# Ten V units of a cached attention in five transfers of 8 MB, with K in two slots of its own

## The chip, the cores and the metric

The kernel runs on one core of one Trainium2 chip. The metric is the device time of one execution in microseconds (us). A profile of one execution lies beside the times; line numbers such as L694 are lines of the kernel before.

## The reference

Two blocks read the same eight rows `x` (8 x 576) and are mixed by a gate. Block A is attention with one query per sequence over the last 2048 keys of a cache; block B is a layer norm, a 576 to 4608 projection, a GELU and the projection back.

```python
g = sigmoid((x * gate_w).sum(-1))
q = (x @ wq).reshape(8, 1, 32, 128)                 # 32 query heads, 16 K/V heads
k = repeat(k_cache[:, :, 8192 - 2048:, :], 2)       # 8 x 16 heads x 2048 keys x 128
v = repeat(v_cache[:, :, 8192 - 2048:, :], 2)
p = softmax(q @ k.T * 128 ** -0.5)
a = (p @ v).reshape(8, 4096) @ wo
h = gelu(layernorm(x) @ w1 + b1)
b = h @ w2 + b2
out = g * a + (1 - g) * b
```

All is bf16 in memory. The window of K and of V is 67 MB each; the weights are about 20 MB.

## The kernel before

**Units.** K and V are each read in 16 units of 4 MB. Unit n belongs to group g = n // 4 (32 of the 128 pairs of sequence and K/V head) and holds 512 of the 2048 keys of these pairs. In SBUF a unit is 128 partitions x 32 KB: four partitions per pair, 128 keys in each. The kernel walks through four groups of four units and rescales a running sum `O` from unit to unit; at the end of a group the accumulated result is reduced and written into a matrix that the output projection reads.

**Slots.** `RAW` has `ND = 4` slots of 32 KB per partition. `take_slot` deals them out in the turn 1, 2, 0, 3, to K and V alike. `load_item` (L623 to L630) issues one transfer on SP's queue, which waits for `slot_free[s]`: for a K unit its four transposes, for a V unit its PV matmuls. The order of transfers is `stream` (L590 to L594 and L603): K0 K1 V0 K2 V1 K3 V2 ... K15 V14 V15, then the weights of the last projections. The first weights lie in slots 0 and 3 and are read before.

**A K unit** (`k_unit`). Four times (a "quarter" below, `tr` and `qk` in the code): VectorE transposes 128 x 2048 words (L694) into one of two buffers in `KT`, and PE adds eight matmuls (L712 and L175) to four banks of scores, in which a mask lies already. The transpose of a quarter waits for the matmuls of the second quarter before it, whose buffer it takes.

**Softmax** (`softmax`, `spread`). VectorE takes the maximum (L645) and the bias (L647, L649), ScalarE makes the exponentials P (L651), and then writes the mask into the banks for the next unit (L655). VectorE transposes P into one of two halves of `PT` (L669). At the end of a group a short chain of small steps forms the sums (L675 to L682).

**A V unit** (`v_item`). POOL and ScalarE copy P into a matrix with zeros between ("spread P", L743 and L744: `qrx`), whose one home lies at the end of `RAW`; unit 15 uses `KT`, which is cleared for that (L727). Then PE runs 64 matmuls (`pv`: L757, and L186 in a loop with registers), and VectorE adds the result to `O` (L798, L800: `o`). After the last unit of a group it forms the group's result (L803, L806, L808: `vmul`, `acc`, `ew`) and PE adds it to a bank (L811: `us`).

**What sets the order.** Each engine's instructions stand in a fixed order, written by the planner `_Plan.schedule`: it takes the operations by estimated start, from the costs that are given with each, and from a model of the transfers (`DMA_BW`, `DMA_LAT`). At run time every operation waits for its `deps` by semaphores, in that order; `after` only acts on the planner.

**The end.** Behind V15 come b2, 3.4 MB of w2, wo in two transfers and the rest of w2 (L833, L850, L862). Their matmuls (L583) all add to one bank, which is written out at L892 to L897.

Of the kernel before, what the change touches and what calls it, by code (L numbers as in the profile page):

```python
# [6 lines left out]
BF = mybir.dt.bfloat16  # L7
# [30 lines left out]

class _Plan:

    DMA_BW = 428e3
    DMA_LAT = 1.8
    DMA_ISSUE = 0.35
    SEM_LAT = 0.08

# [16 lines left out]
    def schedule(self):  # L62
        n = len(self.all)
        done = [False] * n
        eng_free = {e: 0.0 for e in ENGS}
        dma_free = 0.0
        remaining = set(range(n))
        npred = [0] * n
        succ = [[] for _ in range(n)]
        for op in self.all:  # L70
            preds = set(d.idx for d in op.deps) | set(d.idx for d in op.after)
            npred[op.idx] = len(preds)
            for p in preds:
                succ[p].append(op.idx)
        ready = [i for i in range(n) if npred[i] == 0]
        count = 0
        while ready:
            best = None
            best_key = None
            for i in ready:  # L80
                op = self.all[i]
                r = 0.0
                for d in op.deps:
                    r = max(r, d.t1 + self.SEM_LAT)
                for d in op.after:
                    r = max(r, d.t0)
                est = max(eng_free[op.eng], r)
                key = (est - 0.2 * op.prio, -op.prio, i)
                if best_key is None or key < best_key:
                    best_key = key  # L90
                    best = i
            op = self.all[best]
            ready.remove(best)
            est = max([eng_free[op.eng]] + [d.t1 + self.SEM_LAT for d in op.deps] + [d.t0 for d in op.after])
            op.t0 = est
            if op.is_dma:
                eng_free[op.eng] = est + op.cost
                if op.nbytes < 65536:
                    op.t1 = est + 0.4 + self.DMA_LAT
                else:  # L100
                    start = max(est + 0.4, dma_free)
                    dma_free = start + op.nbytes / self.DMA_BW
                    op.t1 = dma_free + self.DMA_LAT
            else:
                op.t1 = est + op.cost
                eng_free[op.eng] = op.t1
            op.pos = len(self.order[op.eng])
            self.order[op.eng].append(op)
            done[best] = True
            count += 1  # L110
            for s_ in succ[best]:
# [12 lines left out]
        for e in ENGS:  # L124
            for op in self.order[e]:
                if op.is_dma:
                    cnts[op.dma_sem] = cnts.get(op.dma_sem, 0) + 1
                    op.dma_val = 16 * cnts[op.dma_sem]
        needed = set()
        for op in self.all:  # L130
            for d in op.deps:
                if not d.is_dma:
                    needed.add(d.idx)
        for e in ENGS:
            c = 0
# [57 lines left out]
def build_kernel(nc, A_x, A_k_cache, A_v_cache, A_wq, A_wo, B_x, B_w1, B_b1, B_w2, B_b2, gate_w, out):  # L193
# [22 lines left out]
    WO_CH = 16  # L216
    JN = D // NJ
    BIG = 1.0e9
    x2 = A_x.rearrange("b s d -> (b s) d")
    out2 = out.rearrange("b s d -> (b s) d")  # L220

    with ExitStack() as es:
# [15 lines left out]
        req("ones_bf", 512, BF)  # L238
        req("zeros_bf", 128, BF)
        req("maskL", 128, BF)  # L240
        req("maskR", 512, BF)
# [8 lines left out]
        req("pair", 128, F32)  # L250
        req("selv", 136, F32)
        req("maskhd", 4, F32)
        req("r8", 128, F32)
        req("idf8", 8, F32)
        req("dg", 16, F32)
        req("sel", 4 * 128, BF)
        req("sel4", 128, BF)
        req("cols", 16, F32)
        req("xT", 6 * 32, BF)
        req("yT", 6 * 32, BF)  # L260
        req("q4", 4 * 256, BF)
        req("qbd", 4 * 4 * 128, BF)
        req("b2", D, BF)
        req("uh", FCW, F32)
        req("v1", FCW, F32)
        req("hT", FT * 32, BF)
        req("ob", 16, BF)
        req("ot32", 8, F32)
# [1 line left out]
        req("sm", 8 * NL, F32)  # L270
        req("sg", 8 * NG, F32)
        req("gcol", 1, F32)
        req("on", 512, BF)
        req("O", 256, F32)
        req("EW", 512, F32)
        req("EV", 128, F32)
        req("oT", 512, BF)
        req("out_sb", JN, BF)
# [4 lines left out]
        over("vm", "uh", 0, 256, F32)  # L283
        over("x_sb", "PT", 0, D, BF)
        over("gw_sb", "PT", 1152, D, BF)
        over("y_bf", "PT", 2304, D, BF)
# [64 lines left out]
        EV, Oc = view("EV"), view("O")  # L351
        RAW = view("RAW")
        PX = aoffs("RAW") + ND * DE
        ptx_f = bass.AP(arena_f, offset=PX // 2, ap=[[AST // 2, 128], [1, 4096]])
        x_sb, gw_sb, y_bf = view("x_sb", 8), view("gw_sb", 8), view("y_bf", 8)
        xz = view("xz", 8).rearrange("p (s c) -> p s c", s=2)
        yz = view("yz", 8).rearrange("p (s c) -> p s c", s=2)
# [3 lines left out]
        def slot(s):  # L361
            return RAW[:, s * DE:(s + 1) * DE]
# [248 lines left out]
        pt_done, px_done, pv_done = {}, {-1: [o_px0]}, {}  # L611
# [4 lines left out]
        px_engs = [("pool", "pool", "act", "act")] * (NL - 2) + [("act", "dve", "dve", "dve"), ("act", "dve", "dve", "dve")]  # L616

        def take_slot():
            n = n_slot[0]
            n_slot[0] += 1  # L620
            return (1, 2, 0, 3)[n % ND]

        def load_item(cache, nm, n):  # L623
            s = take_slot()
            g, i = divmod(n, 4)
            src = cache.rearrange("b h s d -> (b h) s d")[32 * g:32 * g + 32, S0 + KL * i:S0 + KL * i + KL, :].rearrange("j (x r) d -> j x (r d)", x=4)
            d = dma("sp", lambda e: e.dma_start(slot(s), src), "s%d" % s, 8 * W * Dh * 2, deps=slot_free[s], name="%s%d" % (nm, n), after=last_dma[-1:])
            last_dma.append(d)
            slot_free[s] = []
            return s, d  # L630

        def query(g):
            qb_done[g] = []
# [52 lines left out]
        def k_unit(n, s, d):  # L686
            g, i = divmod(n, 4)
            trs = []
            for rh in range(2):
                for hh in range(2):  # L690
# [33 lines left out]
            if n == NL - 1:  # L724
                o_kz.deps.append(qk)

        o_kz = add("pool", lambda e: e.memset(view("KT").bitcast(F32), 0.0), deps=[], name="ktx0", cost=4.5, prio=3)  # L727

        def v_item(n):
            s, d = load_item(A_v_cache, "dv", n)  # L730
            g, i = divmod(n, 4)
            if n == NL - 1:
                spread(n)
            ob_ = BK_OS[n % 2]
            px_at = aoffs("KT") if n == NL - 1 else PX
            px_free = [o_kz] if n == NL - 1 else [pv_done.get(n - 1), o_px0]
            px_done[n] = []
            for c in range(4):
                def fn(e, c=c):
# [6 lines left out]

            if n == NL - 2:
                mx_done[n + 1].after.extend(op for op in px_done[n] if op.eng == "dve")
                o_kz.deps.extend(op for op in px_done[n] if op.eng == "dve")

            def pv_part(a, b):
                def fn(e):
# [30 lines left out]
            if n >= NL - 2:  # L783
                after.append(keep_warm("warm_pv%d" % n, (10, 6)[n - NL], after, (ob_,), [o_u, o_done[n - 2]]))
            if n < NL - 1:
                pv = add("pe", lambda e: pv_looped(e, 64, 2, 6 if n < NL - 2 else 12), deps=deps, name="pv%d" % n, cost=8.2, after=after)
            else:
                pva = add("pe", lambda e: pv_looped(e, 48, 4, 14), deps=deps, name="pv%da" % n, cost=5.4, after=after)
# [4 lines left out]
            slot_free[s] = [pv]  # L793
# [89 lines left out]
        pv_hist = []  # L883
        query(0)
        for kind, i in stream:
            {"K": k_item, "V": v_item, "W": wo_all, "M": m2_chunk, "B": bias}[kind](i)

        acc_ops = [g_.op for g_ in acc_groups]
        fin = []
# [61 lines left out]
```

## Time and profile before

| | before |
|---|---|
| median of 3 runs | 364.59 us (364.51 to 364.76) |
| the profiled execution | 364.57 us |
| its span | 363.3 us |
| mean granted TensorE clock | 0.92 |
| busy: PE, DVE, ACT, POOL | 78%, 71%, 36%, 20% of the span |
| moved by the DMA engines | 154.45 MB, mean 425 GB/s |
| K and V transfers | 16 + 16 of 4096 KB, 26.4 and 26.3 us from issue to landing (median) |
| chain that ended last, by engine | DMA 50%, DVE 35%, PE 9%, issue 4%, ACT 2% |

The span runs from the first to the last instruction; the execution's own time is 1.27 us longer. The time from issue to landing holds the wait in the queue behind earlier transfers. The clock is that which the chip granted to TensorE, 1.00 or 0.50 in any moment.

### The profile page before, as it was taken

Reading aid. Unit: us, or ns where it says so; the run is one execution under the profiler, and the core shown is the slowest. Engines: PE = TensorE matmul, PEld = TensorE weight load, DVE = VectorE, ACT = ScalarE, POOL = GpSimd, SP = SyncE. Lnnn points to the kernel's source line nnn. Section 1 sums busy time; section 2 is a strip of 40 time slices with the busy share of each in tenths; the row PEclk is TensorE's granted clock in tenths of the full one; section 3 lists DMA queues with packets and bytes.
Section 4 is the critical chain, followed back from the end, with each engine's and each line's share of the span. In section 5 each row is a group of like instructions: output and inputs, shape, how many; then the busy total and the mean of one; then the engine's idle time right before and its main releaser. Section 6 shows DMA issues by size and latency. Waiting matters only on the chain.

```text
span 363.3 us, 4428 instructions
## 1 busy us (share of the span) xinstructions
PE 284.4 (78%) x1842; PEld 126.6 (35%) x1381; DVE 257.3 (71%) x201; ACT 131.8 (36%) x117; POOL 73.5 (20%) x72
## 2 busy tenths in 40 slices
PE   0355554999897967997978949897969679978996
PEld 0110000436171703452432607170706034513763
DVE  0722978797978596959495878677695979498530
ACT  1012106274544440735342434444444416313300
POOL 9123002230414040302212030404040403003000
PEclk9976596999998997999896998998999899999999
DMA  8999999999999999999999999999999999999995
GB/s 349 433 440 402 462 404 459 404 462 404 462 404 460 404 462 408 456 411 451 413 451 415 451 415 451 415 451 413 447 419 451 415 451 412 449 415 447 412 440 234
DMA packets 6146, 154.45 MB, mean 425 GB/s; under 512 B 716, under 2 KB 884, under 8 KB 1272
## 3 DMA queue, kind: packets, MB, share of 16 engines
q1 hardware_dynamic: 6080, 154.29, 98.7%
q8 instruction: 6, 0.10, 0.1%
q10 hardware_dynamic: 56, 0.03, 0.0%
q14 instruction: 4, 0.03, 0.0%
HBM read 154.31 MB, written 0.01 MB: 425 GB/s over the span
## 4 chain that ended last, share of the span: by engine, by line
DMA 50%; DVE 35%; PE 9%; issue 4%; ACT 2%; ACTq 0%; POOL 0%; SPq 0%
DMA arena<-in_A_k_cache_dram 42%; DVE arena L694 20%; DMA arena<-in_B_w_dram 5%; DVE arena L669 5%; PE ps L175 4%; DMA arena<-in_gate_w_dram 2%; DVE arena L645 2%; PE ps L186 2%; DVE arena L803 1%; PE ps L505 1%; PE ps L712 1%; DVE arena L800 1%; DVE arena L566 1%; DVE arena L808 1%; ACT arena L651 1%
## 5 line engine op out<-in xcount | busy, mean ns | idle before, releaser
L694 DVE STREAM_TRANSPOSE arena<-arena 128x2048 f32<-128x2048 f32 x64 | 145.0, 2288 | 23.6 <-DMA arena<-in_A_k_cache_dram 20.9
L175 PE MATMUL ps<-arena 128*128 128x512 bf16 (+2 forms) x461 | 131.2, 436 | 0.0
L186 PE MATMUL ps<-arena 128*128 x942 | 106.1, 274 | 0.1
L712 PE MATMUL ps<-arena 128*128 128x512 bf16 x128 | 54.6, 426 | 54.4 <-DVE arena L694 47.7
L186 PEld LDWEIGHTS ps<-arena 128*128 x942 | 92.4, 98 | 11.6 <-issue 0.6
L744 POOL COPY arena<-arena 32x2048 bf16<-32x2048 bf16 x28 | 52.8, 1884 | 211.1 <-DVE arena L669 210.3
L743 ACT ACTIVATE arena<-arena 32x2048 bf16<-32x2048 bf16 x30 | 57.2, 1906 | 64.3 <-DVE arena L669 64.0
L651 ACT ACTIVATE arena<-ps,arena 128x2048 bf16<-128x2048 f32 x16 | 31.5, 1967 | 113.1 <-DVE arena L649 78.5
L712 PEld LDWEIGHTS ps<-arena 128*128 128x128 bf16 x128 | 13.5, 105 | 159.0 <-DVE arena L694 98.1
L645 DVE TENSOR_REDUCE arena<-ps 128x1 f32<-128x2048 f32 x16 | 36.7, 2292 | 35.4 <-PE ps L175 35.4
L669 DVE STREAM_TRANSPOSE arena<-arena 128x2048 bf16<-128x2048 bf16 x16 | 36.4, 2274 | 2.1 <-ACT arena L651 2.1
L655 ACT ACTIVATE ps<-arena 128x2048 f32<-128x2048 f32 x15 | 28.1, 1873 | 0.1
L757 PE MATMUL ps<-arena 128*128 128x256 bf16 x82 | 14.5, 276 | 1.0 <-DVE arena L744 1.0
L757 PEld LDWEIGHTS ps<-arena 128*128 128x128 bf16 x82 | 8.0, 100 | 19.0 <-issue 17.1
L455 PE MATMUL ps<-arena 8*128 8x8 bf16 x8 | 0.6, 171 | 14.6 <-DVE arena L429 9.5
L583 PE MATMUL ps<-arena 128*8 128x288 bf16 (+1 forms) x140 | 9.6, 286 | 1.6 <-DMA arena<-in_A_wo_dram 0.6
L561 DVE TENSOR_TENSOR arena<-arena 128x1152 f32<-128x1152 f32 x1 | 1.4, 1358 | 11.5 <-ACT arena L559 11.5
L727 POOL MEMSET arena<- 128x4096 f32 x1 | 3.5, 3510 | 22.7 <-DVE arena L744 22.7
L583 PEld LDWEIGHTS ps<-arena 128*8 128x8 bf16 (+1 forms) x140 | 5.7, 86 | 5.9 <-DMA arena<-in_B_w_dram 1.3
L638 POOL COPY arena<-arena 32x128 bf16<-32x128 bf16 x16 | 4.6, 287 | 15.0 <-ACT arena L540 7.4
L429 DVE COPY arena<-arena 8x64 bf16<-8x64 bf16 x2 | 0.3, 190 | 9.1 <-DMA arena<-in_gate_w_dram 9.1
L800 DVE SCALAR_TENSOR_TENSOR arena<-arena,ps 128x256 f32<-128x256 f32 x12 | 5.3, 446 | 1.4 <-PE ps L757 1.4
(106 smaller groups left out, 98.9 us busy)
## 6 DMA issues: line engine op xcount, KB each, us to landing
arena<-in_A_k_cache_dram SPq DMA_DIRECT2D x16, 4096.0 KB, 26.4
arena<-in_A_v_cache_dram SPq DMA_DIRECT2D x16, 4096.0 KB, 26.3
arena<-in_B_w_dram SPq DMA_DIRECT2D x1, 4608.0 KB, 23.3
arena<-in_A_wo_dram SPq DMA_DIRECT2D x2, 2304.0 KB, 20.6
arena<-in_A_wq_dram SPq DMA_DIRECT2D x1, 4096.0 KB, 12.9
arena<-in_B_w_dram SPq DMA_DIRECT2D x1, 3456.0 KB, 26.6
arena<-in_B_w_dram SPq DMA_DIRECT2D x1, 1152.0 KB, 19.6
arena<-in_B_w_dram SPq DMA_DIRECT2D x1, 576.0 KB, 24.2
```

The source lines that it names most:

```text
L175: return e.add_instruction(mybir.InstMatmult(name=nc.get_next_instruction_name(), engine=mybir.EngineType.PE, ins=[e.lower_ap(rhs), e.lowe ...
L186: return e.add_instruction(mybir.InstMatmult(name=nc.get_next_instruction_name(), engine=mybir.EngineType.PE, ins=[operand(r, r_ap), opera ...
L583: ins = e.matmul(ps[32 * j:32 * j + 8, BK_ACC, 0:JN], lhsT, rhs[:, JN * j:JN * j + JN], start=False, stop=True, skip_group_check=True, til ...
L645: mx = mx_done[n] = add("dve", lambda e: e.tensor_reduce(out=k(n, MX), in_=ps[:, 0:4, :].rearrange("p a n -> p (a n)"), axis=AXL.X, op=ALU ...
L651: ex = add("act", lambda e: e.activation(out=Pm, in_=ps[:, 0:4, :].rearrange("p a n -> p (a n)"), func=ACTF.Exp, bias=k(n, NB), scale=SCAL ...
L655: mask_done[n + 1] = add("act", lambda e: e.activation(out=ps[:, 0:4, :].rearrange("p a (n c) -> p (a n) c", c=32), in_=bass.AP(arena_f, o ...
L669: pt_done[n] = add("dve", lambda e: e.transpose(bass.AP(arena, offset=aoffs("PT") + 2048 * (n % 2), ap=[[AST, 128], [1, 2048]]), Pm), deps ...
L694: tr = add("dve", (lambda rh=rh, hh=hh, kb=kb: lambda e: e.transpose(bass.AP(arena_f, offset=foffs("KT") + kb * 2048, ap=[[AST // 2, 128], ...
L712: mm = e.matmul(*args, start=False, stop=True, skip_group_check=True) if rc == 0 else held_matmul(nc, e, *args, stop=True, skip=True)
L743: return e.activation(out=dst, in_=src, func=ACTF.Copy)
L744: return e.tensor_copy(dst, src)
L757: mm = e.matmul(ps[:, ob_, 0:256], lhsT, rhs, start=(k == 0), stop=True, skip_group_check=True)
```

## The change

Ten of the sixteen V units, 2 to 11, come in five transfers of two units each (`P2`, `P4`, `P6`, `P8`, `P10`): 128 partitions x 64 KB into slots 2 and 3 together. Such a transfer waits for the PV matmuls of both units that lay there. The partition of the keys follows: a partition holds 256 consecutive keys of a pair, 128 of each of two neighbouring units, so a transfer of one unit now reads every second run of 32 KB. K units use slots 1 and 0 in turn, V units 2 and 3; the turn through four slots is gone. The order of transfers is written out in `STREAM`.

Spread P has two homes, by the parity of the unit, one at the end of `RAW` and one in `PXB`; both are cleared at the start, and the copies of unit n wait for PV n-2 instead of n-1. The clearing of `KT` for unit 15 is gone. To make room, several small tiles share memory. The planner's model of transfers and the costs of `qk` and `pv` have other numbers, and the loop body of two PVs near the end is 6 matmuls long instead of 12 and 14.

```diff
-    DMA_BW = 428e3
-    DMA_LAT = 1.8
+    DMA_BW = 433.2e3
+    DMA_LAT = 0.45
+    DMA_START = 1.7
...
-                    start = max(est + 0.4, dma_free)
+                    start = max(est + self.DMA_START, dma_free)
...
+    STREAM = "K0 K1 V0 K2 V1 K3 K4 P2 K5 K6 P4 K7 K8 P6 K9 K10 P8 K11 K12 P10 K13 K14 V12 V13 K15 V14 V15"
...
+        req("PXB", SE, BF)
...
-        ptx_f = bass.AP(arena_f, offset=PX // 2, ap=[[AST // 2, 128], [1, 4096]])
+        PXS = (PX, aoffs("PXB"))
...
-        stream = [("K", 0), ("K", 1)]
-        for vi in range(NL):
-            stream.append(("V", vi))
-            if vi + 2 < NL:
-                stream.append(("K", vi + 2))
+        stream = [(k[0], int(k[1:])) for k in STREAM.split()]
...
-        o_px0 = add("pool", lambda e: e.memset(ptx_f, 0.0), deps=[o_qp, o_hp], name="ptx0", cost=4.5)
-        n_slot = [0]
+        px_zero = [add("pool", (lambda k=k: lambda e: e.memset(bass.AP(arena_f, offset=PXS[k] // 2, ap=[[AST // 2, 128], [1, 4096]]), 0.0))(), deps=[o_qp, o_hp] + [o_hf] * k, name="ptx%d" % k, cost=4.5) for k in range(2)]
+        late_slots = [1, 0, 2]
...
-        def load_item(cache, nm, n):
-            s = take_slot()
+        def load_item(cache, nm, n, s, both=False):
             g, i = divmod(n, 4)
-            src = cache.rearrange("b h s d -> (b h) s d")[32 * g:32 * g + 32, S0 + KL * i:S0 + KL * i + KL, :].rearrange("j (x r) d -> j x (r d)", x=4)
-            d = dma("sp", lambda e: e.dma_start(slot(s), src), "s%d" % s, 8 * W * Dh * 2, deps=slot_free[s], name="%s%d" % (nm, n), after=last_dma[-1:])
+            keys = cache.rearrange("b h s d -> (b h) s d")[32 * g:32 * g + 32, S0 + 2 * KL * (i // 2):S0 + 2 * KL * (i // 2) + 2 * KL, :]
+            if both:
+                src, dst = keys.rearrange("j (x r) d -> j x (r d)", x=4), RAW[:, s * DE:(s + 2) * DE]
+            else:
+                src, dst = keys.rearrange("j (x u r) d -> u j x (r d)", x=4, u=2)[n % 2], slot(s)
+            free = slot_free[s] + (slot_free[s + 1] if both else [])
+            d = dma("sp", lambda e: e.dma_start(dst, src), "s%d" % s, (1 + both) * 8 * W * Dh * 2, deps=free, name="%s%d" % (nm, n), after=last_dma[-1:])
...
-                    qk = add("pe", qk_fn, deps=deps, name="qk%d_%d%d" % (n, rh, hh), cost=1.85, after=qk_half[-1:] + pv_hist[-1:])
+                    qk = add("pe", qk_fn, deps=deps, name="qk%d_%d%d" % (n, rh, hh), cost=1.75, after=qk_half[-1:] + pv_hist[-1:])
...
         def v_item(n):
-            s, d = load_item(A_v_cache, "dv", n)
+            v_unit(n, 2 + n % 2, load_item(A_v_cache, "dv", n, 2 + n % 2))
+
+        def v_pair(n):
+            d = load_item(A_v_cache, "dv", n, 2, both=True)
+            for u in range(2):
+                v_unit(n + u, 2 + u, d)
+
+        def v_unit(n, s, d):
...
-            px_at = aoffs("KT") if n == NL - 1 else PX
-            px_free = [o_kz] if n == NL - 1 else [pv_done.get(n - 1), o_px0]
+            px_at = PXS[n % 2]
+            px_free = [pv_done.get(n - 2), px_zero[n % 2]]
...
-                pv = add("pe", lambda e: pv_looped(e, 64, 2, 6 if n < NL - 2 else 12), deps=deps, name="pv%d" % n, cost=8.2, after=after)
+                pv = add("pe", lambda e: pv_looped(e, 64, 2, 6), deps=deps, name="pv%d" % n, cost=7.1, after=after)
...
         def k_item(n):
-            s, d = load_item(A_k_cache, "dk", n)
-            k_unit(n, s, d)
+            s = 1 - n % 2
+            k_unit(n, s, load_item(A_k_cache, "dk", n, s))
```

More of the change, by code (lines that the diff above doesn't have):

```diff
@@ L98, in schedule @@
                 if op.nbytes < 65536:
-                    op.t1 = est + 0.4 + self.DMA_LAT
+                    op.t1 = est + 0.4 + 1.8
                 else:
-                    start = max(est + 0.4, dma_free)
+                    start = max(est + self.DMA_START, dma_free)
                     dma_free = start + op.nbytes / self.DMA_BW
@@ L237, in build_kernel @@
         req("ident", 128, BF)
-        req("ones_bf", 512, BF)
+        req("EW", 512, F32)
+        over("ones_bf", "EW", 0, 512, BF)
+        over("sel", "EW", 1024, 4 * 128, BF)
         req("zeros_bf", 128, BF)
@@ L252, in build_kernel @@
         req("maskhd", 4, F32)
-        req("r8", 128, F32)
         req("idf8", 8, F32)
         req("dg", 16, F32)
-        req("sel", 4 * 128, BF)
         req("sel4", 128, BF)
         req("cols", 16, F32)
-        req("xT", 6 * 32, BF)
-        req("yT", 6 * 32, BF)
+        req("early", 640, BF)
+        over("xT", "early", 0, 6 * 32, BF)
+        over("yT", "early", 384, 6 * 32, BF)
+        over("r8", "early", 768, 128, F32)
+        over("b2", "early", 0, D, BF)
         req("q4", 4 * 256, BF)
         req("qbd", 4 * 4 * 128, BF)
-        req("b2", D, BF)
-        req("uh", FCW, F32)
-        req("v1", FCW, F32)
+        req("vm", 256, F32)
+        req("PXB", SE, BF)
+        over("uh", "PXB", 0, FCW, F32)
+        over("v1", "PXB", 4 * FCW, FCW, F32)
         req("hT", FT * 32, BF)
@@ L272, in build_kernel @@
         req("gcol", 1, F32)
-        req("on", 512, BF)
         req("O", 256, F32)
-        req("EW", 512, F32)
         req("EV", 128, F32)
-        req("oT", 512, BF)
-        req("out_sb", JN, BF)
         req("PT", 2 * 2048, BF)
@@ L282, in build_kernel @@
         req("RAW", ND * DE + SE, BF, 512)
-        over("vm", "uh", 0, 256, F32)
+        over("on", "P", 0, 512, BF)
+        over("oT", "P", 1024, 512, BF)
+        over("out_sb", "PT", 0, JN, BF)
         over("x_sb", "PT", 0, D, BF)
@@ L606, in build_kernel @@
         slot_free = [[o_qp], [], [], [o_hp]]
-        o_px0 = add("pool", lambda e: e.memset(ptx_f, 0.0), deps=[o_qp, o_hp], name="ptx0", cost=4.5)
-        n_slot = [0]
+        px_zero = [add("pool", (lambda k=k: lambda e: e.memset(bass.AP(arena_f, offset=PXS[k] // 2, ap=[[AST // 2, 128], [1, 4096]]), 0.0))(), deps=[o_qp, o_hp] + [o_hf] * k, name="ptx%d" % k, cost=4.5) for k in range(2)]
+        late_slots = [1, 0, 2]
         tr_hist, qk_half = [], []
         qk_unit, qb_done = {}, {}
-        pt_done, px_done, pv_done = {}, {-1: [o_px0]}, {}
+        pt_done, px_done, pv_done = {}, {}, {}
         ex_done, nb_done, al_done, ss_done, o_done = {}, {}, {}, {}, {}
@@ L618, in take_slot @@
         def take_slot():
-            n = n_slot[0]
-            n_slot[0] += 1
-            return (1, 2, 0, 3)[n % ND]
-        def load_item(cache, nm, n):
-            s = take_slot()
-            g, i = divmod(n, 4)
-            src = cache.rearrange("b h s d -> (b h) s d")[32 * g:32 * g + 32, S0 + KL * i:S0 + KL * i + KL, :].rearrange("j (x r) d -> j x (r d)", x=4)
-            d = dma("sp", lambda e: e.dma_start(slot(s), src), "s%d" % s, 8 * W * Dh * 2, deps=slot_free[s], name="%s%d" % (nm, n), after=last_dma[-1:])
+            return late_slots.pop(0)
+        def load_item(cache, nm, n, s, both=False):
+            g, i = divmod(n, 4)
+            keys = cache.rearrange("b h s d -> (b h) s d")[32 * g:32 * g + 32, S0 + 2 * KL * (i // 2):S0 + 2 * KL * (i // 2) + 2 * KL, :]
[5 more added lines that the diff above has]
+            d = dma("sp", lambda e: e.dma_start(dst, src), "s%d" % s, (1 + both) * 8 * W * Dh * 2, deps=free, name="%s%d" % (nm, n), after=last_dma[-1:])
             last_dma.append(d)
             slot_free[s] = []
-            return s, d
+            if both:
+                slot_free[s + 1] = []
+            return d
         def query(g):
@@ L723, in k_unit @@
             softmax(n)
-            if n == NL - 1:
-                o_kz.deps.append(qk)
-        o_kz = add("pool", lambda e: e.memset(view("KT").bitcast(F32), 0.0), deps=[], name="ktx0", cost=4.5, prio=3)
         def v_item(n):
-            s, d = load_item(A_v_cache, "dv", n)
+            v_unit(n, 2 + n % 2, load_item(A_v_cache, "dv", n, 2 + n % 2))
[4 more added lines that the diff above has]
+        def v_unit(n, s, d):
             g, i = divmod(n, 4)
@@ L748, in v_item @@
                 mx_done[n + 1].after.extend(op for op in px_done[n] if op.eng == "dve")
-                o_kz.deps.extend(op for op in px_done[n] if op.eng == "dve")
             def pv_part(a, b):
@@ L785, in v_item @@
             if n < NL - 1:
-                pv = add("pe", lambda e: pv_looped(e, 64, 2, 6 if n < NL - 2 else 12), deps=deps, name="pv%d" % n, cost=8.2, after=after)
+                pv = add("pe", lambda e: pv_looped(e, 64, 2, 6), deps=deps, name="pv%d" % n, cost=7.1, after=after)
             else:
-                pva = add("pe", lambda e: pv_looped(e, 48, 4, 14), deps=deps, name="pv%da" % n, cost=5.4, after=after)
+                pva = add("pe", lambda e: pv_looped(e, 48, 4, 6), deps=deps, name="pv%da" % n, cost=5.4, after=after)
                 sums[g].after.append(pva)
@@ L792, in v_item @@
             pv_done[n] = pv
-            slot_free[s] = [pv]
+            slot_free[s] = slot_free[s] + [pv]
             al = sm[:, n, 3:4]
@@ L885, in build_kernel @@
         for kind, i in stream:
-            {"K": k_item, "V": v_item, "W": wo_all, "M": m2_chunk, "B": bias}[kind](i)
+            {"K": k_item, "V": v_item, "P": v_pair, "W": wo_all, "M": m2_chunk, "B": bias}[kind](i)
         acc_ops = [g_.op for g_ in acc_groups]
```

## The prediction, made before the changed kernel ran

> **What bounds it now.** I read first the slices of the span and the waits of the queue that issues the transfers, then the chain of waits, the order of time around one group's end, and the granted clock by windows. The profiled execution took 364.57 us, its span 363.3; the runs' median is 364.59, so sums against the one hold for the other.
>
> ```profile
> DMA  8999999999999999999999999999999999999995
> ...
> SPq L627 <- DVE arena L694: 114.8, 12, 17.3
> SPq L627 <- PE ps L757: 94.3, 10, 11.4
> ```
>
> The DMA engines are full to the end. SP waits for buffers all the time (us in total, times, longest) and it costs nothing: a 4 MB transfer lands 26.4 us after its issue (page, DMA issues) though it moves for only 9.7. The queue is some 16 us ahead, and that cover hides every late matmul.
>
> ```profile
> 204.10 2.27 DVE arena L694
> 206.37 2.19 DVE arena L669
> 208.57 2.19 DVE arena L694
> 210.76 0.38 DVE arena L800
> 211.16 1.59 DVE arena L803
> 212.77 0.43 DVE arena L806
> 213.23 0.69 DVE arena L808
> 213.92 2.23 DVE arena L694
> ```
>
> In the chain of waits (start, duration) VectorE runs without a gap: K transposes (L694), P's (L669), and at a group's end 2.7 us of accumulation (L803 to L808) ahead of the unit's fourth transpose.
>
> ```profile
> 138.85 0.61 PE L712 MATMUL ps<-arena 128*128 128x512 bf16 x1 [2.99 <-DVE arena L694]
> ...
> 140.53 0.63 PE L712 MATMUL ps<-arena 128*128 128x512 bf16 x1
> ...
> 142.18 2.29 DVE L645 TENSOR_REDUCE arena<-ps 128x1 f32<-128x2048 f32 x1 [3.39 <-PE ps L175]
> 142.84 0.38 PE L757 MATMUL ps<-arena 128*128 128x256 bf16 x2
> ...
> 144.70 1.97 ACT L651 ACTIVATE arena<-ps,arena 128x2048 bf16<-128x2048 f32 x1 [9.61 <-DVE arena L649]
> ...
> 146.84 1.87 ACT L655 ACTIVATE ps<-arena 128x2048 f32<-128x2048 f32 x1
> ...
> 149.82 0.39 PE L712 MATMUL ps<-arena 128*128 128x512 bf16 x1
> ...
> 150.72 0.39 PE L712 MATMUL ps<-arena 128*128 128x512 bf16 x1
> ```
>
> These rows of the timeline are my prices. Four QK matmuls take 0.90 us (149.82 to 150.72), a quarter of a unit (eight) 1.8; the same four took 1.68 at 138.85. A PV takes 7.0 (142.84 to 149.82), exp up to the next mask 2.1 (144.70 to 146.84), the mask 1.9, the maximum 2.3, a transpose 2.2. The handoff from PE to VectorE or SP costs about 0.2, others 0.05 to 0.1.
>
> ```profile
> 131.40:134.90 3.50, 1.43 (x7) 0.19 (x2) 3.46 (x3) 3.48 (x2) 3.44 (x2) 0.99 0.98 421
> 134.90:138.30 3.40, 0.95 (x3) 0.00 (x0) 3.33 (x4) 0.19 (x1) 0.21 (x1) 0.50 0.83 357
> 138.30:141.70 3.40, 2.85 (x7) 0.25 (x2) 0.49 (x1) 0.00 (x0) 0.00 (x0) 0.50 1.05 453
> ```
>
> In the windows (length, PE busy, PEld, DVE, ACT, POOL, clock, DMA) a window of 3.4 us with PE busy for 1.43 is followed by half clock, and a well filled one ends it. Today that also hides behind the queue.
>
> **What the change saves.** In the trace's packets a row of 32 KB takes 1213 ns and one of 36 KB 1364: 151 ns for 4 KB more, so some 5 ns of a row are fixed. Five merged transfers have 8 fewer rows per DMA engine each: 40 x 5 to 9 ns = 0.2 to 0.35 us; I take 0.25. Transfers already follow each other every 9.69 us, 8 x 1.21, so five fewer issues save nothing more. If the chip cuts the rows at 32 KB, the 0.25 is gone.
>
> **What it costs.** A pair overwrites both V slots, so its issue waits for both PVs of the pair before. Those can start only when that pair has landed, with only two K transfers (19.4 us) queued behind it; today each slot has its own wait and 16 us of lead. The transfers behind the issue on SP's queue wait too. K's own slots are free in time: K4, the tightest, waits for K2's transposes, done at 83.1 (today's K4 issue waits for the same at 83.12), and the queue runs dry at about 85. P2 waits for the second PV, done at 92.1 today, against 94.8: no hole. The start of a transfer on an empty queue isn't in the steady part of this trace; the first one, 0.5 MB, landed 3.5 us after issue, of which 1.2 is data, so issue to first byte is between 0 and 2.3. The first packets begin 1.0 after the issue and all engines are at work by 1.25; I take 1.15.
>
> The second home of spread P removes a wait of the copies (L743, L744) for the PV before. In today's timeline they start 0.1 after the transpose L669, so this is worth nothing by itself. It is what lets PV n+1 follow PV n at once; without it 4 us more would stand between them. Moving constants and memsets lies in the first 35 us or on POOL, 20% busy: nothing.
>
> **The loop from one pair to the next.** In the changed program PE's order is: PV 3, K5's four quarters, K6's first three, PV 4, K6's fourth, PV 5. From the end of PV 3 (issue of P4) to that of PV 5 (issue of P6), each step waiting for the one before: K5's first quarter and handoff 2.0; its third transpose, which needs that buffer, 2.2; accumulation of group 0 3.1; fourth transpose 2.2; fourth quarter 2.0; maximum and bias 2.5; exp to mask 2.1; mask 2.0; K6's first quarter 2.0; third transpose 2.2; third quarter 1.8; PV 4 7.0; K6's fourth quarter 1.8; PV 5 and handoff 7.2. Sum 40.1 us. The DMA needs 4 x 9.68 = 38.7 for the same data, so the loop is longer even at full clock.
>
> It isn't at full clock. PE idles 3.5 us ahead of K5's fourth quarter (accumulation and transpose) and 5.6 ahead of K6's first (maximum, exp, mask). By the windows above both start at half clock: 1.5 each, loop 43.1. The next loop, to P8, has no accumulation (-2.7) but the sums' matmul (+0.5), and an idle stretch ahead of K8's first quarter that slows it and part of the second (+2.1): 40.0. The third, to P10, ends a group again: 43.2.
>
> The Trainium skill ("TensorE: Matmul & The Clock Gate", Part 1) says the clock halves after an idle window of about 3.4 us and returns after a busy one. Here a window 41% busy was enough, so the trace decides; by the page alone only the 5.6 us stretches would surely count; two loops would be 1.5 shorter and the time about 376.
>
> Walking the same steps from the start: PV 2 begins at 118.6 (today PE reaches this place at 119.2), P2 having landed at 114.8; PV 3 ends at 132.5. The queue is dry at 133.5 less 1.15 for the start: hole 0.3. PV 5 ends at 132.5 + 43.1 = 175.5 (rounding), the queue is dry at 172.5: hole 4.3. PV 7 at 215.5 against 215.55: 1.3. PV 9 at 258.7 against 255.5: 4.55. Holes 10.5 together. V12 waits for PV 10 alone and has 9 us of cover. But PE is late by then and stays so: two more rounds (40.0 and 36.8) bring PV 13 to 335.5 and the last PV, 29.7 later, to 365.2. Today it ends at 348.8: 16.3 earlier. Behind it today lie 1.24 us of waiting for the last weights (0.63 and 0.61), which vanish: 15.1 late. My walk of today's kernel by the same prices came out up to 1.7 late there, so I take 14.4: 364.6 + 14.4 = **379.0**. What was a transfer bound is then a bound by the loop PE, VectorE, ScalarE.
>
> **Rivals.** (1) The clock stays full, because two PVs back to back fill the windows. Loops 40.1, 38.5, 40.1: PV 3 ends at 129.8, PV 9 at 249.0 against 249.6, one hole of 0.8, and the last PV is 2 us late: **366**. For it: a PV pair is 14 us of dense work. Against: the idle stretches lie between pairs, and today's trace drops the clock in shorter need. (2) The cover holds and the result is not slower: place, the issue of P6; it decides if the loop is at most 38.7 plus the 2.5 us of lead that a full clock leaves at P4. Then only the row saving shows: 364.6 - 0.25 = **364.3**, no change that can be measured (0.2% is about what a measurement here can tell). Against: the sum of 40.1 has little air. If rows are cut in two, it is 364.6 in this case and nothing else changes: the change then doesn't do what it says. (3) A fixed cost for each transfer, which five fewer would save, with the cover holding; from 0.15 us each it shows as faster. For it, nothing in rows: 9.69 between landings is eight rows. The Trainium skill ("DMA: Bandwidth & Descriptors", Anatomy of one DMA) gives 2.0 us fixed per transfer, by which it would be 10 less, 354.6; the trace disagrees for queued transfers.
>
> **How the numbers follow.** My forecast, 0.80, spans 373 to 384: the half clock may strike one stretch per loop (-1.5 x 3, and less at the end) or one window more (+1.7 x 3). A milder form or rival 1, 366 to 373: 0.10. Rival 2: 0.05. Rival 3: 0.05. The range that holds 8 in 10 runs from 371 to 384. Faster 0.05, within 0.2% 0.05, slower 0.90.
>
> **What would show it.** Right: DMA slices under 9 at about 175, 215 and 259 us; SP waiting for the PV matmuls just before them; PV pairs with one quarter between; half clock at 141 to 155 us; TensorE at work without a wait for the last weights. The merged rows should take 2.42 us. Wrong: full DMA slices throughout, or a loop under 39 us between pair issues, or holes ahead of K transfers.

## The result, and the profile after

| | before | changed |
|---|---|---|
| median of 6 runs | 364.55 us (364.43 to 364.76) | 377.10 us (375.61 to 378.25) |
| ratio to before, 95% interval | | 1.0342 [1.0320, 1.0364] |
| the profiled execution, its span | 364.57, 363.3 us | 377.11, 375.8 us |
| mean granted clock | 0.92 | 0.914 |
| moved | 154.45 MB, mean 425 GB/s | 154.45 MB, mean 411 GB/s |

The change is slower by 12.5 us. Line numbers from here on are those of the changed kernel, one to six higher: L698 is the K transpose, L716 and L176 the scores, L763 and L187 the PV, L629 the issue of K and V.

The page's slices and its chain of waits by engine (before: DMA 50%, DVE 35%, PE 9%):

```profile
PE 40%; DVE 40%; DMA 13%; ACT 4%; issue 2%; ACTq 0%; POOL 0%; SPq 0%
...
DMA  8999999999999999898999989997999999999995
```

A slice is 9.4 us; from the seventeenth on four are no longer full, around 155, 174, 221 and 258 us, and the chain now runs through PE and VectorE. What SP waited for:

```profile
SPq L629 <- DVE arena L698: 139.9, 11, 28.7
SPq L629 <- PE ps L763: 104.2, 8, 16.2
```

These waits tell nothing by themselves: in total they are only some 10 to 25 us longer than before. What matters is how early the issue comes behind such a wait. I call **lead** the time from the issue to the moment when the transfers ahead of it are through (the landing ahead less 0.6 us), and **loss** what lies between two landings above the 9.69 us per 4 MB of the undisturbed rows:

| transfer | issued | lead | loss |
|---|---|---|---|
| K4 | 83.1 | 1.9 | 0.70 |
| P2 | 92.1 | 3.3 | 1.21 |
| P4 | 132.9 | 2.4 | 0.40 |
| P6 | 173.8 | 0.6 | 3.15 |
| P8 | 214.1 | 2.2 | 1.83 |
| K12 | 243.0 | 4.3 | 0.26 |
| P10 | 258.2 | -0.9 | 3.65 |
| V13, V14 | 297.7, 318.9 | 11.8, 10.5 | 0.53, 0.89 |

All losses, net and with those near the start, are 14.0 us, against 1.5 in the kernel before. The difference, 12.5, is the difference of the spans: the slowdown is time in which data came too slowly, and nothing else. V13 and V14 were issued early enough; their losses belong to the last section, as does a part of P2's.

The loop that made the issues late, in the chain of waits (start, duration, what), from K5's third transpose to the landing of P6:

```profile
134.71 2.31 DVE arena L698
...
139.10 2.23 DVE arena L698
141.38 0.40 PE ps L716
...
143.39 2.30 DVE arena L649
...
145.91 2.06 ACT arena L655 x2
...
148.15 1.78 ACT ps L659
...
150.07 0.59 PE ps L716
150.65 1.28 PE ps L176 x3
...
167.03 6.55 PE ps L187 x60
...
173.82 23.69 DMA arena<-in_A_v_cache_dram
```

That is the prediction's walk: transpose, fourth quarter, maximum, exponentials, mask, K6's quarters, both PVs, issue of P6. P4 landed only at 155.7, so neither of its PVs could stand in the stretch from 144.2 to 150.1, where PE waits for the softmax. Windows (length, PE busy, PEld, DVE, ACT, POOL, clock, DMA share, GB/s) over this stretch and around P6's issue; the last two count a row whole in the window in which it starts, so that a share can be above 1:

```profile
137.48:140.89 3.41, 1.57 (x7) 0.10 (x1) 3.34 (x4) 0.00 (x0) 0.00 (x0) 1.00 1.38 596
...
144.30:147.70 3.40, 0.00 (x0) 0.00 (x0) 3.37 (x3) 1.79 (x1) 0.00 (x0) 1.00 1.25 540
147.70:151.10 3.40, 1.03 (x3) 0.10 (x1) 3.40 (x3) 2.53 (x5) 0.00 (x0) 0.51 0.89 386
151.10:154.60 3.50, 3.50 (x9) 0.29 (x2) 2.31 (x2) 2.06 (x2) 2.00 (x2) 0.51 0.81 349
171.00:173.00 2.00, 2.00 (x21) 1.79 (x19) 2.00 (x2) 2.00 (x4) 0.00 (x0) 1.00 0.87 377
173.00:175.00 2.00, 2.00 (x15) 0.66 (x7) 2.00 (x2) 0.68 (x2) 0.00 (x0) 1.00 0.35 147
175.00:177.00 2.00, 1.94 (x9) 0.19 (x2) 2.00 (x2) 1.03 (x1) 1.00 (x1) 1.00 1.59 524
```

A window with PE busy for 1.57 us leaves the clock full. One with PE idle is followed by two at half clock, where K6's first matmul takes 0.59 us instead of 0.39. At P6 rows for only 147 GB/s start from 173 to 175. Spread over the time that each row takes, the trace's packets give 256 GB/s there, 232 and 345 in the two windows behind, and 433 when nothing is late. No row at all is in work for only 0.51 us; at P10's hole it is 1.97 us. The rest of the losses lies in engines that wait singly and in slow first rows. On the 16 DMA engines P6's first rows start 1.3 to 2.4 us after the issue, and they take 2.9 to 3.5 us, where the usual 64 KB row takes 2.42.

### The profile page after: what moved, and what is told of

The parts are those of the page before. It is cut to its first block, busy times and chain, and to the rows that moved or that the text cites. A ratio compares the mean times of both kernels' runs of the same rounds, so it can differ in the third digit from the quotient of the medians.

```text
span 375.8 us, 4420 instructions
## 1 busy us (share of the span) xinstructions
PE 282.7 (75%) x1827; PEld 124.5 (33%) x1381; DVE 256.6 (68%) x201; ACT 131.8 (35%) x117; POOL 73.6 (20%) x72
## 2 busy tenths in 40 slices
DMA packets 5426, 154.45 MB, mean 411 GB/s; under 512 B 636, under 2 KB 804, under 8 KB 1192
## 4 chain that ended last, share of the span: by engine, by line
PE 40%; DVE 40%; DMA 13%; ACT 4%; issue 2%; ACTq 0%; POOL 0%; SPq 0%
DVE arena L698 23%; PE ps L187 18%; PE ps L176 14%; DMA arena<-in_A_v_cache_dram 6%; DVE arena L649 6%; DMA arena<-in_B_w_dram 5%; PE ps L716 4%; DVE arena L673 4%; DMA arena<-in_gate_w_dram 2%; ACT arena L655 2%; ACT ps L659 1%; PE ps L763 1%; PE ps L509 1%; DVE arena L809 1%; DVE arena L570 1%
## 5 line engine op out<-in xcount | busy, mean ns | idle before, releaser
L698 DVE STREAM_TRANSPOSE arena<-arena 128x2048 f32<-128x2048 f32 x64 | 145.0, 2290 | 12.2 <-PE ps L176 12.0
L176 PE MATMUL ps<-arena 128*128 128x512 bf16 (+2 forms) x456 | 131.5, 437 | 21.0 <-DVE arena L698 17.9
L187 PE MATMUL ps<-arena 128*128 x942 | 106.0, 273 | 0.0
L187 PEld LDWEIGHTS ps<-arena 128*128 x942 | 89.9, 98 | 13.9 <-issue 1.2
L716 PE MATMUL ps<-arena 128*128 128x512 bf16 x119 | 51.0, 428 | 41.8 <-DVE arena L698 21.3
L716 PEld LDWEIGHTS ps<-arena 128*128 128x128 bf16 x128 | 13.4, 105 | 164.1 <-issue 89.8
L763 PE MATMUL ps<-arena 128*128 128x256 bf16 x82 | 14.1, 272 | 1.4 <-DVE arena L751 0.9
L763 PEld LDWEIGHTS ps<-arena 128*128 128x128 bf16 x82 | 7.8, 99 | 18.7 <-issue 14.2
L804 DVE COPY arena<-ps 128x256 f32<-128x256 f32 x4 | 1.6, 404 | 11.4 <-PE ps L763 11.4
L607 POOL MEMSET arena<- 128x4096 f32 x2 | 7.0, 3512 | 10.0 <-DVE arena L569 5.5
L679 PE MATMUL ps<-arena 128*128 128x1 f32 x8 | 1.8, 298 | 7.7 <-DVE arena L653 7.7
```

Source lines behind the costliest of these rows:

```text
L176: return e.add_instruction(mybir.InstMatmult(name=nc.get_next_instruction_name(), engine=mybir.EngineType.PE, ins=[e.lower_ap(rhs), e.lowe ...
L187: return e.add_instruction(mybir.InstMatmult(name=nc.get_next_instruction_name(), engine=mybir.EngineType.PE, ins=[operand(r, r_ap), opera ...
L698: tr = add("dve", (lambda rh=rh, hh=hh, kb=kb: lambda e: e.transpose(bass.AP(arena_f, offset=foffs("KT") + kb * 2048, ap=[[AST // 2, 128], ...
L716: mm = e.matmul(*args, start=False, stop=True, skip_group_check=True) if rc == 0 else held_matmul(nc, e, *args, stop=True, skip=True)
L763: mm = e.matmul(ps[:, ob_, 0:256], lhsT, rhs, start=(k == 0), stop=True, skip_group_check=True)
```

## Experiments

All times are medians beside the kernel before on the same chip (364.5 to 364.75 us).

**split.** The five pairs become ten transfers of 4 MB, each with its own slot's wait; the planner is free.

```diff
-STREAM = "... K4 P2 K5 K6 P4 K7 K8 P6 K9 K10 P8 K11 K12 P10 K13 ..."
+STREAM = "... K4 V2 V3 K5 K6 V4 V5 K7 K8 V6 V7 K9 K10 V8 V9 K11 K12 V10 V11 K13 ..."
```

> Each pair as two 4 MB transfers in 32 KB rows, next to each other in the same order of transfers, each waiting for its own slot and each PV for its own transfer; slots, K's strided rows and the two homes stay. Loop theory (the merged landing comes too late for the first PV to run in the stretch in which PE waits for softmax, so PE's loop is 40 to 43 us where the data need 38.7): the planner puts the first PV back into that stretch, the loop fits, and the time is 365 to 368, by a walk with the trace's durations 365.4. Rival, reads: if K's rows at a pitch of 64 KB or the two slots for K cost the time, it stays at 375 to 378.

370.99 us, 1.0176 [1.0159, 1.0193]: 6.1 us come back, less than expected. The planner now puts a pair's first PV into the softmax stretch. PE, VectorE and ScalarE in the timeline of split:

```profile
144.71 2.29 DVE L649 TENSOR_REDUCE arena<-ps 128x1 f32<-128x2048 f32 x1 [3.27 <-PE ps L176]
...
147.62 0.39 PE L763 MATMUL ps<-arena 128*128 128x256 bf16 x2 [1.66 <-DMA arena<-in_A_v_cache_dram]
148.00 6.93 PE L187 MATMUL ps<-arena 128*128 x60
```

PV 4 starts when its own 4 MB land, beside maximum, exponentials and mask. No V transfer loses more than 0.1 us here. What is left are mainly K transfers that are issued late: with K K V V through two K slots, K4, K6, K10 and K14 have leads of 1.5 to 3.0 us and lose 1.13, 2.04, 1.73 and 2.79 in the profiled execution, which took 373.59 us.

**order.** As split, but PE must run the pair's first PV behind the third quarter of the K unit, as in the changed kernel.

```diff
+third[n] = third.get(n) or (qk if (rh, hh) == (1, 0) else None)      # in k_unit
...
+if 2 <= n <= 10 and n % 2 == 0:                                      # in v_unit
+    after.append(third[n + 2])
...
```

> The same transfers and waits as in the split kernel, but on PE each first PV of a pair is put behind the third quarter of the K unit two ahead, as in the changed kernel. Loop theory: the order on PE alone brings the loss back, 376 to 380 (walk: 378, less some 2 that the walk was too long for the changed kernel). Rival, the queue: if the loss is that one wait covers two slots and one transfer of 8 MB is issued late, this kernel has no such wait and stays within 2 us of the split kernel, 365 to 368.

377.85 us, 1.0367 [1.0349, 1.0384]. The same transfers as split; the order on PE alone costs 6.9 us. The issues of V5, V7, V9 and V11, each of which waits for the PV two units back, now follow each other 43.0, 39.4 and 43.5 us apart; in split it was 38.8, 40.6 and 38.6. In order's timeline of PE the first PV stands behind three quarters (151.84 to 159.63), beside no softmax, and the second behind the fourth:

```profile
159.85 6.71 PE L187 MATMUL ps<-arena 128*128 x60
...
168.63 6.60 PE L187 MATMUL ps<-arena 128*128 x59
```

**rows32.** The merged transfers as they are, but in rows of 32 KB.

```diff
-src, dst = keys.rearrange("j (x r) d -> j x (r d)", x=4), RAW[:, s * DE:(s + 2) * DE]
+src, dst = keys.rearrange("j (x u r) d -> j x u (r d)", x=4, u=2), RAW[:, s * DE:(s + 2) * DE].rearrange("p (u c) -> p u c", u=2)
```

> The changed kernel with the same five 8 MB transfers, waits and orders, but two rows of 32 KB per partition in each in place of one of 64 KB. Loop theory: as the changed kernel, 375.5 to 378.5; the 0.25 us of saved row overhead can't be seen in that spread. Rival, rows: if long rows are slow in themselves, it is faster by several us.

376.74 us, 1.0346 [1.0328, 1.0364]: the length of a row doesn't show.

**alt.** The changed kernel with K slots, homes and strided rows, but K and V in turn as before.

```diff
-STREAM = "K0 K1 V0 K2 V1 K3 K4 P2 ..."
+STREAM = "K0 K1 V0 K2 V1 K3 V2 K4 V3 K5 V4 ... K14 V13 K15 V14 V15"
```

> The changed kernel with the order of transfers of the kernel before (K and V alternating, no pairs), K in slots 1 and 0, V in 2 and 3, two homes of spread P. Loop theory: 364.3 to 365.0, no difference from before. Rival, reads: slower if K's strided rows or K's two slots cost anything; rival, second home: faster if the wait for the PV before had cost anything.

364.67 us, 1.0004 [0.9994, 1.0013]. All that the change does beside merging costs and brings nothing.

**onehome.** Spread P in one home again (unit 15 in the other); its copies wait for the PV before.

```diff
-px_at = PXS[n % 2]
-px_free = [pv_done.get(n - 2), px_zero[n % 2]]
+px_at = PXS[n // (NL - 1)]
+px_free = [pv_done.get(n - 1), px_zero[n // (NL - 1)]]
```

> The changed kernel with one home of spread P for units 0 to 14 (the copies of unit n wait for PV n-1), the second only for unit 15. By the prediction's step, 4 us of copies then stand between the two PVs of every pair: 385 to 389 (walk: 10 more than the changed kernel). Rival: the copies hide beside the K quarter between the PVs and the second home is worth less than 3 us: 377 to 380.

389.56 us, 1.0698 [1.0677, 1.0720]: 12.5 us above the changed kernel. That is a little more than expected. In the traces 4.0 to 4.1 us now stand between the two PVs of every pair. In the changed kernel those of P2 follow each other at once, those of P4 1.7 us apart with a quarter between. At P2 PE only waits for a copy (4.02 us), at P4 it does two quarters and waits 0.48. P4, P6, P8 and P10 lose 5.62, 5.08, 3.03 and 5.48.

**altorder.** alt's transfers with the changed kernel's order on PE (first PV of a pair behind the third quarter of K n+2).

```diff
...
+if 4 <= n <= 12 and n % 2 == 0 and (rh, hh) == (1, 0):
+    pv_done[n - 2].after.append(qk)
...
```

(The other lines give `STREAM` as in alt and let the first three quarters of these units stand ahead of that PV.)

> Alternating single transfers as in the kernel before, K in slots 1 and 0, V in 2 and 3, but PE's order of the changed kernel: PV n (n even, 2 to 10) behind the third quarter of unit n+2, directly ahead of PV n+1. Loop theory: no transfer is merged, each waits for its own slot, and yet the order makes it 374 to 380. Rival, the transfers: with the alternating order 364.3 to 366.

382.23 us, 1.0476 [1.0453, 1.0499], above what was expected: V6 and V10 are issued 3.0 and 1.8 us after the queue ran out and lose 5.64 and 5.93. A late PV makes its slot late, whether the transfers are merged or not.

**lateacc.** A group's accumulation on VectorE goes behind the K unit's fourth transpose.

```diff
+if (rh, hh) == (1, 1) and n % 4 == 1 and n > 4:
+    vm_ops[(n - 5) // 4].after.append(tr)
...
+vm_ops[g] = vmul
...
```

> The changed kernel with a group's accumulation (three VectorE steps, 2.7 us, after units 3, 7 and 11) put behind the fourth transpose of the K unit in hand, not ahead of it. Loop theory: these steps are links of PE's loop, so two to three loops are 2.7 us shorter and the stretch ahead of the fourth quarter vanishes, which also spares a drop of the clock: 368 to 372, holes at the second and fourth pair nearly gone. Rival, the queue's coupling alone (one wait for two slots): VectorE's order has no part in it, 376 to 378.

374.20 us, 1.0251 [1.0220, 1.0281]: 2.9 us, less than expected. All five pair issues now lead by 2.2 to 3.2 us, and still P2 to P10 lose 1.34, 1.58, 0.90, 2.82 and 1.61. P6, P8 and P10 can't lead by much more in this order: from the landing ahead of them to their issue there are at least two PVs and a quarter, 0.2 + 7.0 + 1.8 + 7.0 + 0.2 = 16.2 us (16.3 to 16.5 here), and the two K transfers between cover 19.4 - 0.6 = 18.8.

**warm.** PE's idle stretches in K5 to K12 are filled with matmuls of zeros, which go into a bank that is not in use.

```diff
+FILL = {(1, 1, 1): 11, (2, 0, 0): 20, (0, 0, 0): 24}
...
+fill = FILL.get((n % 4, rh, hh)) if 5 <= n <= 12 else None
+if fill:
+    pre.append(keep_warm(..., fill, ...))      # ahead of the quarter's matmuls
```

> The changed kernel with 11 to 24 matmuls that nobody reads put into the idle stretches of PE in units 5 to 12 (ahead of the fourth quarter after a group's end and of the first quarter of each even unit). Loop theory with the clock: the half clock costs 1.5 to 3 us per loop, three loops and two rounds behind them; filled, 367 to 373 (walk: 369 to 371). Rival, the loop alone, with the clock of no weight: no gain, or slower by up to 2 where the fillings are in the way, 376 to 379.

375.21 us, 1.0279 [1.0257, 1.0301]: 1.9 us, where more was expected. Of five stretches at half clock between 114 and 306 us one is left, at 197.6 to 201.0, on PV 6, which waits for P6's landing. From P2's issue to P10's the loops took 40.1, 40.0, 43.0 and 41.8 us, in the changed kernel 40.8, 40.9, 40.2 and 44.1; the third is the one with that PV. The clock is a small part, and the late issues stay: P6 and P8, with leads of 2.6 and 1.1, lose 2.7 and 2.3.

These runs left one thing disputed: whether a lead of 2 to 3 us is itself a loss, or only goes along with the pairs. The next three take the kernel before, with all its single transfers, its slots and PE's order, and hold back on SP's queue the issues of K7 to K14 until a later operation of VectorE is done.

```diff
+late = [X] if nm == "dk" and 7 <= n <= 14 else []
...
-d = dma(..., deps=slot_free[s], ...)
+d = dma(..., deps=slot_free[s] + late, ...)
```

X is the fourth last transpose for **lead7**, the third last for **lead5**, and for **lead2** the transpose of P two units back (`pt_done[n - 2]`).

> The kernel before with eight K transfers (7 to 14) held back on SP until VectorE has made the first transpose of the K unit that landed last: they are then issued about 6.9 us before the queue runs dry, in place of some 16. Late-start theory (in the runs so far transfers issued with under some 5 us to spare lost 0.3 to 3 us each, though the queue wasn't dry): enough lead, 364.3 to 365.2. Rival (a transfer only has to be issued 1.15 us ahead): the same.

> As the last, but held until the second transpose: 4.6 us of lead. Late-start theory: 0 to 0.7 us lost for each of the eight, 365 to 369. Rival, 1.15 us are enough: 364.3 to 365.2.

> As the last, but held until P's transpose: 2.4 us of lead. Late-start theory: 1 to 2 us for each of the eight, 372 to 380, with PE's order, slots, single transfers and waits as in the kernel before. Rival, 1.15 us are enough: 364.3 to 366.

| | leads of K7 to K14 | time, us | ratio to before | loss of the eight in the profiled execution |
|---|---|---|---|---|
| lead7 | 5.9 to 6.8 | 364.80 | 1.0001 [0.9991, 1.0010] | 0.0 to 0.2 each |
| lead5 | 3.5 to 5.1 | 366.27 | 1.0047 [1.0030, 1.0063] | none |
| lead2 | 2.3 to 2.4 | 375.37 | 1.0289 [1.0220, 1.0358] | 0.42 to 2.86, mean 1.6 |

The last step, some 2 us later on the queue, costs 9 us, and at no moment between K7 and K14 is there no row in work. By the medians lead2 loses 10.6 / 8 = 1.3 us per transfer. lead2's queue at K8 in the timeline of SP, and its windows (columns as above); by the definition of the lead the transfers ahead are through at 173.3:

```profile
170.95 0.53 SPq L628 DMA_DIRECT2D arena<-in_A_k_cache_dram  x1
```

```profile
171.00:173.00 2.00, 0.98 (x4) 0.00 (x0) 2.00 (x1) 1.98 (x2) 1.94 (x2) 0.98 0.99 344
173.00:175.00 2.00, 1.83 (x8) 0.19 (x2) 2.00 (x3) 1.79 (x1) 1.81 (x1) 1.00 0.86 295
175.00:177.00 2.00, 1.39 (x7) 0.19 (x2) 0.70 (x1) 0.00 (x0) 0.00 (x0) 1.00 0.87 360
```

For six us data comes slowly. Spread over the time that each row takes it is 334, 278 and 396 GB/s, where 433 is full, with the DMA engines 81, 91 and 100% busy. There is always a row in work, but not on every engine: V6's last rows, in the trace's packets, end between 171.85 and 173.56 on the 16 engines, 0.9 to 2.6 us after K8's issue, and K8's first row starts 1.32 us after it. So some engines stand idle, 0.56 of the 1.34 us that are missing in these windows, and the other part is slow rows, up to 2.4 us for 32 KB instead of 1.21. (At 181.0 a load of instructions of 0.94 us adds to K8's loss; without K8 and K12, into which such loads fall, the mean of the others is 1.35.) The lead goes by the last engine, and the first ones run dry before. In lead5 the first engine is free 2.0 to 3.3 us after the issue, in lead7 4.7 and more, and neither loses more than 0.2. lead5's extra 1.5 us don't lie in its eight transfers: in the profiled execution V3 and V10, with leads of 10.3 and 11.1, lost 0.94 and 0.60 (see the last section).

**onepair.** alt with a single pair, P6.

```diff
-STREAM = "K0 K1 V0 K2 V1 K3 K4 P2 ..."
+STREAM = "K0 K1 V0 K2 V1 K3 V2 ... K6 V5 K7 K8 P6 K9 V8 K10 V9 K11 V10 ... V14 V15"
```

> The changed kernel's slots, with one pair only (units 6 and 7) and single alternating transfers else. Per-loop theory (each pair's loop costs for itself: loop, clock and late start): one pair, with the two transfers behind it, costs 2 to 4 us, 366.5 to 368.5. Rival: the cover of the alternating order before and after takes one late pair in, 364.4 to 365.2.

368.45 us, 1.0102 [1.0085, 1.0119]: one merged pair costs 3.7 us, and most of it falls on the transfer behind it. P6 itself leads by 7.9 us and loses nothing. V8, which needs PV 6, is issued with 0.2 us to spare and loses 2.32; the next largest loss is V10's 1.25, with a lead of 16.0.

## Why the prediction came out right, and which of its steps did not

The forecast, 379.0, was 1.9 us above the measured 377.1, and the mechanism is the one that it named: the pair's issue waits for both PVs, those wait for a landing that covers both, and the loop between is longer than the data. That the number is so near is in part luck, as its steps show:

- **The walk** of issues held: P4 at 132.9 (132.7 by the walk), P6 173.8 (175.7), P8 214.1 (215.7), P10 258.2 (258.9). The loops were 40.9, 40.3 and 44.1 us, forecast 43.1, 40.0 and 43.2. The first was 2.2 shorter, 1.5 of it by the forecast's own price because the half clock hit once and not twice: K5's fourth quarter (141.38, 0.40 us) ran at full clock, K6's first and half of its second at half. A window 46% busy (1.57 of 3.41) was not enough to lose the clock, one 41% busy had been in the kernel before. The form that the prediction drew from the Trainium skill ("TensorE: Matmul & The Clock Gate", Part 1), that only the long idle stretch surely counts, fits this loop, and its 376 was a little nearer than the 379. It doesn't fit the third loop, where both stretches were followed by half clock (222.8 to 229.7 and 233.1 to 239.9); the window ahead of the first, 219.4 to 222.8, was 29% busy.
- **Holes at the pairs**, forecast 0.3, 4.3, 1.3 and 4.55, 10.5 in all: 0.40, 3.15, 1.83 and 3.65, 9.0 in all. The sum is near by luck. The step "start on an empty queue, 1.15 us" took a lead above 1.15 to be enough, and lead2 shows that 2.3 is not. With the measured issues and landings put in, this step gives 0, 0.6, 0 and 2.1, or 2.7 of the 9.0. The forecast made up for that with later issues (P6 by 1.9 us) against a queue that it took to be dry sooner (172.5; measured 174.4). Behind these issues the first row started 1.32 us or more after the issue, on the last engine 2.4 us or more, and the first rows were slow.
- **"K's own slots are free in time"** failed for that same reason: with a lead of 1.9 K4 lost 0.70, a loss ahead of a K transfer, which the prediction had named as a sign of being wrong. **"P2: no hole"** failed too (1.21), but its cause is less sure: with its lead of 3.3 every engine went on to P2's rows nearly without a wait, the first of them took 2.7 us in the mean instead of 2.42, and a load of instructions of 0.89 us falls into it (last section).
- **The end** is the step that was most off. PE was to set it, 3.9 us beyond the holes (14.4 - 10.5). The last PV ended at 362.2, 3.0 before the walked 365.2, and PE still waits for the last weights in the tail's timeline:

```profile
372.17 1.71 PE L587 MATMUL ps<-arena 128*8 128x288 bf16 x24 [0.58 <-DMA arena<-in_B_w_dram]
```

  V15 and the last weights landed 12.5 us later than before (the weights at 373.5 against 361.0): the end stayed bound by transfers. The losses that the walk lacked (K4, P2, K12, V13, V14: 3.6 us, 0.25 of which V13 lost before too) stand in the place of the 3.9 that did not come; that the two are of a size is luck.
- **The save on rows** can't be seen. The merged rows took 2420 ns as forecast, so they aren't cut, but rows32 is 0.4 us below the changed kernel, inside the spread.
- **The second home** was priced right in kind. "Worth nothing by itself" is what alt shows. The 4 us between the PVs stand in onehome's trace as 4.0 to 4.1. That is 4 more at P2, as priced, but only 0.6 to 2.4 more at the other pairs, where a quarter or two stand between them anyway.
- **Rivals.** Rival 1's condition did not hold, and its price was wrong too: warm, with the clock nearly full over the pairs, saves 1.9 us, not the 11 to its 366. Its loops don't follow from the steps either: 40.1 - 2.7 + 0.5 is 37.9, not 38.5, and 129.8 and its three loops make 248.5, not 249.0. The cover (rival 2) did not hold, and no fixed cost per transfer (rival 3) shows: split and alt have five transfers more and are faster than the changed kernel. The 2.0 us that the prediction names there stand in the Trainium skill ("DMA: Bandwidth & Descriptors", Anatomy of one DMA) for transfers issued from GpSimd; these are issued from SP.

So two things together make most of the loss. A merged landing pushes the first PV of a pair out of the softmax stretch, which lengthens PE's loop past the 38.7 us of data (shown: split against order, 6.9 us, with altorder). And a transfer issued with less than some 3 to 3.5 us to spare starts slowly (shown: lead7, lead5, lead2). Even with the best loop the last three pairs have some 2.6 us to spare, as lateacc shows, so merging over two slots can't get back to the time before in this order of transfers and of work on PE. Merging with more slots wasn't tried. No kernel here beat the one before; alt equals it.

## What to carry to other kernels

A larger transfer lengthens its buffer's loop at both ends: it waits for everything that it overwrites, and it lets its consumers start only when all of it has landed. Before merging, work out the lead that is left (what is queued behind, less the time from landing to the next issue) and look on the consumer's engine for idle time that the earlier landing used to fill. In a kernel bound by transfers look at landings and GB/s, not at whether some row is in work: single DMA engines can be dry or slow, and the slowest one sets the landing.

## What the runs showed of the hardware

- A queued transfer of K or V needs several us of lead. At 5.9 us and more the held-back ones lost at most 0.2. Between 3.5 and 5.5 most lost nothing; six lost 0.7 to 1.4, five of them with a load of instructions in them (next point). Between 1.9 and 3.3 it was 0.4 to 2.9, but for K4 of lateacc and of onehome, which lost nothing. At about 1 and below it was 1.3 to 5.9, the time without any data among it. Two parts of it are seen: the first row of a late transfer starts 1.32 us after the issue at the earliest, and some engines are through with the transfer ahead before that, in lead2's K8 0.9 us after the issue, the last one 2.6. Why the first rows are slow then stays open: no view of these traces parts the making of the rows from the memory's answer.
- A large lead isn't a full guarantee: of the transfers of 2 MB and more issued behind 50 us, 21 with leads above 5.5 us lost 0.4 to 1.5. Beside the rows of data the page has packets of instructions, in the kernel before and the changed one alike:

```profile
q8 instruction: 6, 0.10, 0.1%
q10 hardware_dynamic: 56, 0.03, 0.0%
q14 instruction: 4, 0.03, 0.0%
```

  Each is 8 KB in 0.31 us or 16 KB in 0.9 to 1.2 on one DMA engine. Over all runs 20 of those 21 losses have one between some 2.5 us ahead of the landing before and their own; of 243 such transfers without one a single other lost as much, but 74 with one lost less. In the kernel before the three largest losses behind 50 us (V3 0.39, V10 0.28, V13 0.25) each have one. So they go along with these loads; no run moved a load to prove it.
- A row of 64 KB is moved in one piece, in 2420 ns, twice the 1213 ns of 32 KB less 6.
